# Top-k attention followed by a gated MLP on one core: the attention pipeline one slot shorter, with work moved between VectorE, ScalarE and GpSimd

## The chip, the cores and the metric

The kernel runs on one core of one Trainium2 chip. The metric is the device time of one execution in microseconds (us). The kernel before takes 1711.28 us, the median of three runs that lie between 1711.02 and 1712.13 us. A profile is one further execution, taken by the hardware profiler. The engines are named as in it: PE is TensorE (PEld its weight loads), DVE is VectorE, ACT is ScalarE, POOL is GpSimd, and SP is the queue that issues all DMAs.

## What is computed

Eight batches of eight heads; 576 queries and keys of 64 elements for each head. For every query row only the scores that reach the 32nd largest one count. The result, 4608 rows of 512, goes through a two-layer MLP with the quick GELU. Cut to what matters:

```python
scores = scale * np.matmul(q, k.transpose(0, 1, 3, 2))
kth = np.partition(scores, -top_k, axis=-1)[..., -top_k:-top_k + 1]   # top_k = 32
scores = np.where(scores >= kth, scores, -1000000000.0)
attn = np.exp(scores - np.max(scores, axis=-1, keepdims=True))
attn = attn / (np.sum(attn, axis=-1, keepdims=True) + 1e-09)
o = np.matmul(attn, v)                 # (B,H,S,D) -> x: (B*S, H*D) = 4608 x 512
h = x @ w_in                           # 512 x 2048
g = h * (1.0 / (1.0 + np.exp(-1.702 * h)))
out = g @ w_out                        # 2048 x 512
```

The two weight matrices arrive as 64-bit floats. The kernel turns them into 32-bit floats itself ("rounding" below) from the two 32-bit words of each number; the rest is 32-bit float throughout.

## The kernel before

**Slots.** The attention is cut into 144 slots (`slots`, line 211). A slot is one block of 128 query rows for a pair of heads; each batch has 16 full slots (four row blocks by four head pairs) and two tail slots that share the last 64 rows of two head pairs. The function `slot(n)` (line 445) writes out by hand the order in which every engine gets its work; each engine runs its own queue strictly in that order, and engines wait for each other through semaphores. One call mixes several stages of different slots:

- `scores(n+1)`: PE multiplies queries by keys into `s_ps`, ACT copies the result to `sc` (128 rows, two heads, 576 scores each).
- `topk(n)`: 14 DVE operations, four rounds of "eight largest" (line 245) and three rounds of "remove them" (line 248), each for the two heads. Positions in this list are counted as `i` = 0 to 13 in `slot`.
- `bounds(n-1)`: POOL makes two tiny tiles from the largest and the 32nd largest score. `exponentials(n-1)`: ACT masks the scores (Prelu, line 273), then takes Exp with a running sum `den` (line 275).
- `divide(n-1)`: DVE computes 1/`den` (`some`, `rden`, lines 283 and 285) after position `i` = 5 of `topk(n)`; POOL multiplies the two heads' rows by it (line 288).
- `turn_main(n-2)`, `turn_ends(n-2)`: PE transposes the probabilities in nine blocks into `tp` (line 297), ACT copies them to `pt` (line 298). `values(n-2)`: PE multiplies by V into `o` (line 320), ACT copies to `xT`.
- `prepare`: PE transposes a head pair's queries or keys (lines 199 and 205), ACT copies them to `q_t` or `k_t` (lines 201 to 208). The tables `READY`, `FETCH` and `VALUES` say in which slot of a batch each one is due; around the start of a batch a key pair and the next query pair fall into one slot, twice in each batch from the second on.

**MLP.** When four head pairs of a row block are done, the block joins the list `ready`. Each slot then does a quarter of a block's MLP: `hidden` (16 matmuls, line 361, into the one buffer `ph`), `tanh` on ACT (line 378), `gate` on DVE at the end of the slot's queue (line 385), and in the next slot `project` (four matmuls, line 399), which after four quarters is copied out by ACT (`ob`, line 404) and stored. After the last slot the remaining quarters run alone.

**Weights.** The two weight matrices are loaded and rounded in 32 pieces of 128 by 512 during the first slots: two before slot 0, then three a slot (`by_slot`, line 419). Per piece ACT makes `more` and `size` (lines 133 and 134), DVE runs `cut` (line 137), `sign` (line 142) and `normal` (line 149), and POOL adds the low part (line 146). `cut` and `sign` are put between the operations of `topk(n)`, `normal` after its ninth.

**Buffers.** The tiles `tp` and `o` share two buffers in PSUM (`ps_t`), `s_ps` has two, `ph` and `po` one each. A pool hands out its buffers in turn, so the third `tp` or `o` in program order waits until the first has been copied out.

Of the kernel before, what the change touches and what calls it, by code (L numbers as in the profile page):

```python
# [8 lines left out]
AF = mybir.ActivationFunctionType  # L9
ALU = mybir.AluOpType  # L10
ENG = mybir.EngineType
F32 = mybir.dt.float32
U32 = mybir.dt.uint32
I32 = mybir.dt.int32
PSUM = bass.MemoryType.PSUM

P = 128
TOPK = 32
LOWEST = -3.4028234663852886e38

LEAST_HIGH = 2.0**-15 * 1.125

HUGE = 2.0**100

# [2 lines left out]
def kernel(  # L27
# [24 lines left out]
    nc = tc.nc  # L52
# [11 lines left out]
    G = 4  # L64
    NG = FC // G
    PIECE = 512
    NPIECE = CC * DFF // PIECE + FC
# [6 lines left out]

    const = ctx.enter_context(tc.tile_pool(name="const", bufs=1))
    pool = lambda name, bufs, **kw: ctx.enter_context(tc.tile_pool(name=name, bufs=bufs, **kw))
    raws = pool("raws", 5)
    temps = pool("temps", 3)
    loads = pool("loads", 2)
    vals = pool("vals", 6)  # L80
    qkt = pool("qkt", 5)
# [3 lines left out]
    small = pool("small", 4)  # L85
# [2 lines left out]
    xtt = pool("xtt", 1)  # L88
    gtp = pool("gtp", 3)
    thp = pool("thp", 2)  # L90
    osp = pool("osp", 2)
    ps_s = pool("ps_s", 2, space=PSUM)
    ps_t = pool("ps_t", 2, space=PSUM)
    ps_h = pool("ps_h", 1, space=PSUM)
# [22 lines left out]
    def round_piece(n):  # L117

        c, g = pieces[n]
        dst = wout[:, g, :] if c is None else win[:, c, g * PIECE : (g + 1) * PIECE]
        words = raw.pop(n)[:].rearrange("p (n w) -> p n w", w=2)
        low, high = words[:, :, 0], words[:, :, 1]
        bits = dst.bitcast(U32)  # L130
        more = temps.tile([P, PIECE], I32, name="more")
        size = temps.tile([P, PIECE], F32, name="size")
        nc.scalar.mul(out=more[:], in_=low, mul=2.0**-29)
        nc.scalar.activation(size[:], high.bitcast(F32), AF.Abs)

        def cut():
            nc.vector.tensor_scalar(  # L137
                bits, high, 3, 0x3FFFFFF8, op0=ALU.logical_shift_left, op1=ALU.bitwise_and
            )

        def sign():
            nc.vector.scalar_tensor_tensor(  # L142
                out=bits, in0=high, scalar=0xC0000000, in1=bits, op0=ALU.bitwise_and, op1=ALU.bitwise_or
            )
            whole = dst.bitcast(I32)
            nc.gpsimd.tensor_tensor(out=whole, in0=whole, in1=more[:], op=ALU.add)

        def normal():
            nc.vector.scalar_tensor_tensor(  # L149
                out=dst, in0=size[:], scalar=LEAST_HIGH, in1=dst, op0=ALU.is_ge, op1=ALU.mult  # L150
            )

        return [cut, sign], normal


    qT, kT, vv = {}, {}, {}
# [58 lines left out]
    N = len(slots)  # L215
    PER = N // B
    st = [{} for _ in slots]
# [41 lines left out]
    def bounds(n):  # L259

        top = st[n]["top"]
        cut = st[n]["cut"] = small.tile([P, 2], F32, name="cut")
        low = st[n]["low"] = small.tile([P, 2], F32, name="low")
        nc.gpsimd.tensor_scalar(cut[:], top[:, :, TOPK - 1], -1.0, None, op0=ALU.mult)  # L264
        nc.gpsimd.tensor_tensor(out=low[:], in0=top[:, :, TOPK - 1], in1=top[:, :, 0], op=ALU.subtract)

    def exponentials(n):

        sc, cut, low = st[n]["sc"], st[n]["cut"], st[n]["low"]
        pr = st[n]["pr"] = prp.tile([P, 2 * S], F32, name="pr")  # L270
        den = st[n]["den"] = small.tile([P, 2], F32, name="den")
        for i in range(2):
            nc.scalar.activation(sc[:, i, :], sc[:, i, :], AF.Prelu, bias=cut[:, i : i + 1], alpha=HUGE)  # L273
        for i in range(2):
            nc.scalar.activation(  # L275
                pr[:, i * S : (i + 1) * S], sc[:, i, :], AF.Exp, bias=low[:, i : i + 1],
                accum_out=den[:, i : i + 1],
            )

    def divide(n):  # L280
        den, pr = st[n]["den"], st[n]["pr"]
        some = small.tile([P, 2], F32, name="some")
        nc.vector.tensor_scalar_add(some[:], den[:], 1e-9)
        rden = small.tile([P, 2], F32, name="rden")
        nc.vector.reciprocal(rden[:], some[:])  # L285
        for i in range(2):
            on = pr[:, i * S : (i + 1) * S]
            nc.gpsimd.tensor_scalar(on, on, rden[:, i : i + 1], None, op0=ALU.mult)  # L288

    def turn(n, first, cols, blocks):  # L290
        pr = st[n]["pr"]
# [8 lines left out]
    def turn_main(n):  # L300
        for i in range(2):
            turn(n, i * NF, MAIN[i], NF)

    def turn_ends(n):

        turn(n, 2 * NF, FULL, 1)
# [39 lines left out]

    ready = []
    hidden_at = {"g": 0}
    to_gate, to_project = [], []
    proj = {}  # L350

    def hidden():
# [19 lines left out]

    def tanh():

        if to_gate and len(to_gate[-1]) == 3:
            ph, g, rows = to_gate.pop()
            th = thp.tile([P, G, P], F32, name="th")
            nc.scalar.activation(th[:], ph[:], AF.Tanh, scale=0.851)  # L378
            to_gate.append((ph, g, rows, th))

    def gate():
        if to_gate:
            ph, g, rows, th = to_gate.pop()
            gT = gtp.tile([P, G, P], F32, name="gT")
            nc.vector.scalar_tensor_tensor(  # L385
                out=gT[:], in0=th[:], scalar=1.0, in1=ph[:], op0=ALU.add, op1=ALU.mult
            )
            to_project.append((gT, g, rows))

    def project():  # L390
        if not to_project:
            return
        gT, g, rows = to_project.pop(0)
        if g == 0:
            proj["po"] = ps_p.tile([P, C], F32, name="po")
        po = proj["po"]
        for i in range(G):
            f = g * G + i
            nc.tensor.matmul(  # L399
                po[:], lhsT=gT[:, i, :], rhs=wout[:, f, :], start=(f == 0), stop=(f == FC - 1)  # L400
            )
        if g == NG - 1:
            ob = osp.tile([P, C], F32, name="ob")
            nc.scalar.mul(out=ob[:], in_=po[:], mul=0.5)
            for on, row in rows:
                nc.sync.dma_start(out[row : row + on.stop - on.start, :], ob[on, :])
# [4 lines left out]
    def at(n, fn, *args):  # L411
        later.setdefault(n, []).append((fn, args))
# [3 lines left out]
    READY = ((-6, -5), (-2, -1), (-1, 0), (0, 1))  # L416
    FETCH = ((-12, -11), (-9, -8), (-5, -4), (-1, 0))
    VALUES = (-8, -7, 1, 2)
    by_slot = {-1: [0, 1]}
    for x in range(2, NPIECE):  # L420
        by_slot.setdefault((x - 2) // 3, []).append(x)
    for hp in range(NP):
        for name in "qk":
            at(max(hp - 2, -1), load, name, 0, hp)
            at(hp - 1, prepare, name, 0, hp)
        if hp == 0:
            for x in by_slot[-1]:
                at(-1, load_piece, x)
    for hp in range(NP):
        at(hp - 1, load_v, 0, hp)  # L430
    for n in range(NPIECE // 3):
        for x in by_slot[n]:
            at(n - 1, load_piece, x)
    for b in range(1, B):
        for hp in range(NP):
# [1 line left out]
                at(b * PER + FETCH[hp][i], load, name, b, hp)  # L437
                at(b * PER + READY[hp][i], prepare, name, b, hp)
            at(b * PER + VALUES[hp], load_v, b, hp)
    rounding, last = {}, []  # L440

    def begin_rounding(n):
        rounding[n] = [round_piece(x) for x in by_slot.get(n, [])]

    def slot(n):
        todo = later.pop(n, [])
        for fn, args in todo:
            if fn is not prepare:
                fn(*args)
        if 0 <= n - 1 < N:  # L450
            bounds(n - 1)
            exponentials(n - 1)
        if 0 <= n - 2 < N:
            turn_main(n - 2)
        hidden()
        if 0 <= n - 2 < N:
            turn_ends(n - 2)
        for fn, args in todo:
            if fn is prepare:
                fn(*args)  # L460
        tanh()
        if n + 1 < N:
            scores(n + 1)
        if 0 <= n - 2 < N:
            values(n - 2)
        project()
        if n == -1:
            begin_rounding(-1)
        begin_rounding(n + 1)
        chain = topk(n) if 0 <= n < N else [lambda: None] * 14  # L470
        some = rounding.pop(n)
        first = [op for ops, _ in some for op in ops]
        last.extend(op for _, op in some)
        for i, op in enumerate(chain):
            op()
            if i == 5 and 0 <= n - 1 < N:
                divide(n - 1)
            if i and first:
                first.pop(0)()
            elif last and i > 8:  # L480
                last.pop(0)()
        while first:
            first.pop(0)()
        while last and n >= 0:
            last.pop(0)()
        gate()

    with tc.manual_schedule():
        for n in range(-1, N + 2):
            slot(n)  # L490
        n = N + 2
        while ready or to_project:
            slot(n)
            n += 1

# [29 lines left out]
```

## Time and profile before

| what | value |
|---|---|
| three runs, median | 1711.28 us |
| the profiled execution, its own time | 1710.55 us |
| span of the profiled execution | 1708.6 us |
| granted TensorE clock, mean | 0.97 |
| DVE busy | 1581.2 us (93%) |
| ACT busy | 989.5 us (58%) |
| POOL busy | 595.1 us (35%) |
| DVE "eight largest", lines 245 | 864 and 288 operations of some 746 ns |
| DVE "remove", line 248 | 864 operations of 742 ns |
| DVE gate, line 385 | 144 operations of 671 ns |
| POOL division, line 288 | 288 operations of 1723 ns |
| ACT Prelu and Exp, lines 273 and 275 | 288 each, 767 and 761 ns |

Busy times of an engine overlap little but not never: an operation's duration includes a fixed part that the next one can hide, so the distance between two starts is shorter than a duration (a DVE "eight largest" starts 0.67 us after the one before). The span runs from the first to the last recorded instruction; the execution's own time is 1.95 us longer.

### The profile page before, as it was taken

The page shows a single profiled execution, that of the slowest core. Times are in us where ns is not written, and L with a number is a line of the kernel's source. Part 1 is how long each engine was busy: PE and PEld are TensorE (multiplying, and loading weights), DVE is VectorE, ACT ScalarE, POOL GpSimd, SP SyncE. Part 2 cuts the span into 40 slices and gives each one's busy share as a digit, 9 for nine tenths or more (in the row PEclk, how much of TensorE's full clock was granted, in tenths as well). Part 3 has the DMA queues.
Part 4 walks back from the last instruction along what each step waited for, and adds up shares of the span by engine and source line. Part 5 has one row for each costly group of instructions (what it writes and reads, how often), then busy time and mean ns, then how long its engine had stood idle before and what let it go on. Part 6 is the DMA issues. An engine that isn't in the chain of part 4 may idle for free.

```text
span 1708.6 us, 31456 instructions
## 1 busy us (share of the span) xinstructions
PE 1604.8 (94%) x11824; PEld 1183.7 (69%) x11824; DVE 1581.2 (93%) x3408; ACT 989.5 (58%) x2149; POOL 595.1 (35%) x620
## 2 busy tenths in 40 slices
PE   3447899899999999999999999999999999999998
PEld 2336677577777777777777777777777777777776
DVE  7999999999999999999999999999999999899940
ACT  5655566556665566556665566556665565655530
POOL 3454333333323333333333333333333333233320
PEclk8568999999999999999999999999999999999999
DMA  8232001101000101011000101010010100000000
GB/s 234 93 108 78 20 21 29 42 1 28 21 21 21 35 21 35 14 35 29 21 21 21 35 21 35 14 35 21 21 29 21 35 21 21 22 7 8 7 7 13
DMA packets 125718, 56.54 MB, mean 33 GB/s; under 512 B 116864, under 2 KB 116864, under 8 KB 125568
## 3 DMA queue, kind: packets, MB, share of 16 engines
q1 hardware_dynamic: 125568, 54.55, 12.2%
q8 instruction: 93, 1.52, 0.4%
q14 instruction: 57, 0.47, 0.1%
HBM read 45.09 MB, written 9.44 MB: 32 GB/s over the span
## 4 chain that ended last, share of the span: by engine, by line
PE 87%; DVE 11%; SPq 1%; ACT 1%; issue 0%; DMA 0%; DVEq 0%
PE po L399 29%; PE ph L361 29%; PE o L320 10%; PE s_ps L229 9%; PE tp L297 8%; DVE top L245 4%; DVE left L248 3%; PE tp L199 2%; DVE wout L149 1%; DVE wout L142 1%; DVE win L149 1%; DVE win L137 1%; ACT k_t L201 0%; DVE wout L137 0%; DVE win L142 0%
## 5 line engine op out<-in xcount | busy, mean ns | idle before, releaser
L288 POOL TENSOR_SCALAR pr<-pr,rden 128x576 f32<-128x576 f32 x288 | 493.0, 1723 | 688.1 <-DVE rden L285 427.0
L245 DVE MAX8 top<-left 128x8 f32<-128x576 f32 x864 | 610.1, 746 | 0.0
L399 PE MATMUL po<-wout,gT 128*128 128x512 f32 x1152 | 532.0, 605 | 0.0
L361 PE MATMUL ph<-xT,win 128*128 128x128 f32 x4096 | 489.5, 279 | 18.4 <-DVE gT L385 18.4
L361 PEld LDWEIGHTS ph<-xT,win 128*128 128x128 f32 x4096 | 478.3, 196 | 20.7 <-DVE gT L385 19.7
L248 DVE MATCH_REPLACE8 left<-top,left 128x576 f32<-128x576 f32 x576 | 423.5, 742 | 0.0
L399 PEld LDWEIGHTS po<-wout,gT 128*128 128x128 f32 x1152 | 207.1, 189 | 229.0 <-issue 227.7
L273 ACT ACTIVATE sc<-sc,cut 128x576 f32<-128x576 f32 x288 | 207.3, 767 | 207.0 <-POOL cut L264 207.0
L298 ACT COPY pt<-tp 128x512 f32<-128x512 f32 (+1 forms) x432 | 188.7, 470 | 227.6 <-PE tp L297 227.2
L297 PEld LDWEIGHTS tp<-ident,pr 128*128 128x128 f32 x1296 | 157.3, 143 | 129.4 <-issue 62.1
L297 PE MATMUL tp<-ident,pr 128*128 128x128 f32 x1296 | 195.1, 278 | 50.6 <-ACT pt L298 37.7
L275 ACT ACTIVATE pr<-sc,low 128x576 f32<-128x576 f32 x288 | 218.8, 761 | 0.0
L248 DVE MATCH_REPLACE8 left<-top,sc 128x576 f32<-128x576 f32 x288 | 211.7, 742 | 0.0
L245 DVE MAX8 top<-sc 128x8 f32<-128x576 f32 x288 | 203.5, 747 | 0.9
L236 ACT COPY sc<-s_ps 128x576 f32<-128x576 f32 x288 | 170.4, 645 | 55.2 <-PE s_ps L229 53.2
L229 PE MATMUL s_ps<-k_t,q_t 64*128 64x288 f32 (+1 forms) x1280 | 187.4, 440 | 0.9 <-ACT k_t L201 0.9
L320 PEld LDWEIGHTS o<-pt,v_l 128*64 128x64 f32 x2560 | 130.2, 139 | 57.5 <-ACT th L378 36.3
L320 PE MATMUL o<-pt,v_l 128*64 128x128 f32 (+1 forms) x2560 | 164.4, 272 | 0.0
L385 DVE SCALAR_TENSOR_TENSOR gT<-th,ph 128x512 f32<-128x512 f32 x144 | 96.6, 671 | 54.1 <-ACT th L378 53.8
L264 POOL TENSOR_SCALAR cut<-top 128x2 f32<-128x2 f32 x144 | 31.9, 222 | 304.5 <-DVE top L245 304.5
L229 PEld LDWEIGHTS s_ps<-k_t,q_t 64*128 64x128 f32 (+1 forms) x1280 | 102.1, 181 | 41.0 <-issue 20.6
L378 ACT ACTIVATE th<-ph 128x512 f32<-128x512 f32 x144 | 87.1, 605 | 35.6 <-PE ph L361 35.6
(41 smaller groups left out, 786.0 us busy)
## 6 DMA issues: line engine op xcount, KB each, us to landing
q_l<-in_q_dram SPq DMA_DIRECT2D x64, 128.0 KB, 2.5
k_l<-in_k_dram SPq DMA_DIRECT2D x64, 128.0 KB, 2.5
raw<-in_moe_w_in_dram SPq DMA_DIRECT2D x16, 512.0 KB, 4.2
v_l<-in_v_dram SPq DMA_DIRECT2D x64, 128.0 KB, 2.5
raw<-in_moe_w_out_dram SPq DMA_DIRECT2D x16, 512.0 KB, 3.8
out_dram<-ob SPq DMA_DIRECT2D x32, 256.0 KB, 2.1
ends<-in_q_dram SPq DMA_DIRECT2D x32, 32.0 KB, 2.2
ends<-in_k_dram SPq DMA_DIRECT2D x32, 32.0 KB, 2.3
```

What stands on the lines that cost most here:

```text
L229: nc.tensor.matmul(ps[i][rows, c, 0:HALF], lhsT=qT[b, hps[p]][on, cols], rhs=kT[b, hps[p]][on, FIRST[i] + c * HALF : FIRST[i] + (c + 1) * ...
L236: nc.scalar.copy(out=sc[:, i, :].rearrange("p (c k) -> p c k", c=2), in_=ps[i][:, :, 0:HALF])
L245: nc.vector.max(top[:, i, 8 * r : 8 * r + 8], (left if r else sc)[:, i, :])
L248: nc.vector.match_replace(left[:, i, :], top[:, i, 8 * r : 8 * r + 8], (left if r else sc)[:, i, :], LOWEST)
L273: nc.scalar.activation(sc[:, i, :], sc[:, i, :], AF.Prelu, bias=cut[:, i : i + 1], alpha=HUGE)
L275: nc.scalar.activation(pr[:, i * S : (i + 1) * S], sc[:, i, :], AF.Exp, bias=low[:, i : i + 1], accum_out=den[:, i : i + 1],)
L288: nc.gpsimd.tensor_scalar(on, on, rden[:, i : i + 1], None, op0=ALU.mult)
L297: nc.tensor.transpose(tp[:, c * P : (c + 1) * P], pr[:, cols + c * P : cols + (c + 1) * P], ident[:])
L298: nc.scalar.copy(out=to, in_=tp[:, 0 : blocks * P])
L320: nc.tensor.matmul(o[j * D : (j + 1) * D, 0 : cols.stop - cols.start], lhsT=main[:, c, j, :] if c < NF else tail[:, j, :], rhs=pt[:, j * N ...
L361: nc.tensor.matmul(ph[:, i, :], lhsT=win[:, c, f * P : (f + 1) * P], rhs=xT[:, c, :], start=(c == 0), stop=(c == CC - 1),)
L399: nc.tensor.matmul(po[:], lhsT=gT[:, i, :], rhs=wout[:, f, :], start=(f == 0), stop=(f == FC - 1))
```

## The change

The pipeline loses one slot: transposes and `values` handle slot n-1 instead of n-2, and the order inside `slot` is rewritten. `exponentials(n)` now stands at the end of slot n, and the inversion of `den` after position 8 of `topk(n+1)`. The multiplication by 1/`den` moves from POOL to ACT. `gate` moves from DVE to POOL as two operations, on copies of both factors that ACT makes. `normal` is dropped: `size` is bounded below by a POOL operation first, and `cut` reads it instead of the raw word; the low part is written over the raw piece. Pieces go four a slot for six slots, then three for two. `prepare` of the first batch is one slot earlier, and in every slot it follows `scores`. `project` is split in two halves around `turn_ends`.

```diff
-LEAST_HIGH = 2.0**-15 * 1.125
+LEAST_HIGH = 2.0**-15
...
-    raws = pool("raws", 5)
-    temps = pool("temps", 3)
+    raws = pool("raws", 6)
+    temps = pool("temps", 4)
...
-    osp = pool("osp", 2)
+    osp = pool("osp", 1)
...
-        more = temps.tile([P, PIECE], I32, name="more")
         size = temps.tile([P, PIECE], F32, name="size")
-        nc.scalar.mul(out=more[:], in_=low, mul=2.0**-29)
+        nc.scalar.mul(out=low.bitcast(I32), in_=low, mul=2.0**-29)
         nc.scalar.activation(size[:], high.bitcast(F32), AF.Abs)
+        nc.gpsimd.tensor_scalar(size[:], size[:], LEAST_HIGH, None, op0=ALU.max)
         def cut():
             nc.vector.tensor_scalar(
-                bits, high, 3, 0x3FFFFFF8, op0=ALU.logical_shift_left, op1=ALU.bitwise_and
+                bits, size[:].bitcast(U32), 3, 0x3FFFFFF8, op0=ALU.logical_shift_left, op1=ALU.bitwise_and
             )
...
-            nc.gpsimd.tensor_tensor(out=whole, in0=whole, in1=more[:], op=ALU.add)
-        def normal():
-            nc.vector.scalar_tensor_tensor(
-                out=dst, in0=size[:], scalar=LEAST_HIGH, in1=dst, op0=ALU.is_ge, op1=ALU.mult
-            )
-        return [cut, sign], normal
+            nc.gpsimd.tensor_tensor(out=whole, in0=whole, in1=low.bitcast(I32), op=ALU.add)
+        return [cut, sign]
...
-            nc.gpsimd.tensor_scalar(on, on, rden[:, i : i + 1], None, op0=ALU.mult)
+            nc.scalar.activation(on, on, AF.Copy, scale=rden[:, i : i + 1])
...
+            h = thp.tile([P, G, P], F32, name="h")
+            nc.scalar.copy(out=h[:], in_=ph[:])
...
-            nc.vector.scalar_tensor_tensor(
-                out=gT[:], in0=th[:], scalar=1.0, in1=ph[:], op0=ALU.add, op1=ALU.mult
-            )
+            nc.gpsimd.tensor_tensor(out=gT[:], in0=th[:], in1=h[:], op=ALU.mult)
+            nc.gpsimd.tensor_tensor(out=gT[:], in0=gT[:], in1=h[:], op=ALU.add)
...
-        for i in range(G):
+        for i in range(part * G // 2, (part + 1) * G // 2):
...
+    RATES = (2, 4, 4, 4, 4, 4, 4, 3, 3)
...
-            at(max(hp - 2, -1), load, name, 0, hp)
-            at(hp - 1, prepare, name, 0, hp)
+            at(max(hp - 3, -1), load, name, 0, hp)
+            at(max(hp - 2, -1), prepare, name, 0, hp)
```

The body of `slot` after the change (it replaces lines 446 to 486; `invert` is the part of `divide` that makes `rden`):

```python
        before = 0 <= n - 1 < N
        chain = topk(n) if 0 <= n < N else [lambda: None] * 14
        more = rounding.pop(n, [])
        for i, op in enumerate(chain):
            op()
            if i and more:
                more.pop(0)()
            if i == 8 and before:
                invert(n - 1)
        for op in more:
            op()
        if before:
            divide(n - 1)
        if n == -1:
            for args in preparing[:2]:
                prepare(*args)
            del preparing[:2]
        if n + 1 < N:
            scores(n + 1)
        for args in preparing:
            prepare(*args)
        hidden()
        if before:
            turn_main(n - 1)
        tanh()
        project(0)
        if before:
            turn_ends(n - 1)
        project(1)
        if n == -1:
            for op in begin_rounding(-1):
                op()
        rounding[n + 1] = begin_rounding(n + 1)
        if before and n <= len(by_slot):
            values(n - 1)
        if 0 <= n < N:
            bounds(n)
            exponentials(n)
        gate()
        if before and n > len(by_slot):
            values(n - 1)
```

More of the change, by code (lines that the diff above doesn't have):

```diff
@@ L278, in exponentials, with invert, divide @@
             )
-    def divide(n):
-        den, pr = st[n]["den"], st[n]["pr"]
+    def invert(n):
+        den = st[n]["den"]
         some = small.tile([P, 2], F32, name="some")
         nc.vector.tensor_scalar_add(some[:], den[:], 1e-9)
-        rden = small.tile([P, 2], F32, name="rden")
+        rden = st[n]["rden"] = small.tile([P, 2], F32, name="rden")
         nc.vector.reciprocal(rden[:], some[:])
+    def divide(n):
+        pr, rden = st[n]["pr"], st[n]["rden"]
         for i in range(2):
             on = pr[:, i * S : (i + 1) * S]
-            nc.gpsimd.tensor_scalar(on, on, rden[:, i : i + 1], None, op0=ALU.mult)
+            nc.scalar.activation(on, on, AF.Copy, scale=rden[:, i : i + 1])
     def turn(n, first, cols, blocks):
@@ L348 @@
     hidden_at = {"g": 0}
-    to_gate, to_project = [], []
+    to_gate, gated, to_project = [], [], []
     proj = {}
@@ L373, in tanh @@
     def tanh():
-        if to_gate and len(to_gate[-1]) == 3:
+        if to_gate:
             ph, g, rows = to_gate.pop()
@@ L378, in tanh, with project @@
             nc.scalar.activation(th[:], ph[:], AF.Tanh, scale=0.851)
-            to_gate.append((ph, g, rows, th))
+            h = thp.tile([P, G, P], F32, name="h")
+            nc.scalar.copy(out=h[:], in_=ph[:])
+            gated.append((th, h, g, rows))
     def gate():
-        if to_gate:
-            ph, g, rows, th = to_gate.pop()
+        if gated:
+            th, h, g, rows = gated.pop()
             gT = gtp.tile([P, G, P], F32, name="gT")
-            nc.vector.scalar_tensor_tensor(
-                out=gT[:], in0=th[:], scalar=1.0, in1=ph[:], op0=ALU.add, op1=ALU.mult
-            )
+            nc.gpsimd.tensor_tensor(out=gT[:], in0=th[:], in1=h[:], op=ALU.mult)
+            nc.gpsimd.tensor_tensor(out=gT[:], in0=gT[:], in1=h[:], op=ALU.add)
             to_project.append((gT, g, rows))
-    def project():
-        if not to_project:
+    def project(part):
+        if not to_project or (part and not proj.get("begun")):
             return
-        gT, g, rows = to_project.pop(0)
-        if g == 0:
+        gT, g, rows = to_project[0]
+        if g == 0 and part == 0:
             proj["po"] = ps_p.tile([P, C], F32, name="po")
+        proj["begun"] = True
         po = proj["po"]
-        for i in range(G):
+        for i in range(part * G // 2, (part + 1) * G // 2):
             f = g * G + i
@@ L401, in project @@
             )
+        if part == 0:
+            return
+        to_project.pop(0)
+        proj["begun"] = False
         if g == NG - 1:
@@ L418 @@
     VALUES = (-8, -7, 1, 2)
-    by_slot = {-1: [0, 1]}
-    for x in range(2, NPIECE):
-        by_slot.setdefault((x - 2) // 3, []).append(x)
+    RATES = (2, 4, 4, 4, 4, 4, 4, 3, 3)
+    by_slot, x = {}, 0
+    for n, rate in enumerate(RATES, -1):
+        by_slot[n] = list(range(x, x + rate))
+        x += rate
+    assert x == NPIECE
     for hp in range(NP):
         for name in "qk":
-            at(max(hp - 2, -1), load, name, 0, hp)
-            at(hp - 1, prepare, name, 0, hp)
+            at(max(hp - 3, -1), load, name, 0, hp)
+            at(max(hp - 2, -1), prepare, name, 0, hp)
         if hp == 0:
@@ L430 @@
         at(hp - 1, load_v, 0, hp)
-    for n in range(NPIECE // 3):
+    for n in range(len(by_slot) - 1):
         for x in by_slot[n]:
@@ L439 @@
             at(b * PER + VALUES[hp], load_v, b, hp)
-    rounding, last = {}, []
+    rounding = {}
     def begin_rounding(n):
-        rounding[n] = [round_piece(x) for x in by_slot.get(n, [])]
+        return [op for x in by_slot.get(n, []) for op in round_piece(x)]
     def slot(n):
         todo = later.pop(n, [])
+        preparing = [args for fn, args in todo if fn is prepare]
         for fn, args in todo:
@@ L449, in slot @@
                 fn(*args)
[L450 to L461, printed above, removed]
+        before = 0 <= n - 1 < N
+        chain = topk(n) if 0 <= n < N else [lambda: None] * 14
+        more = rounding.pop(n, [])
+        for i, op in enumerate(chain):
+            op()
+            if i and more:
+                more.pop(0)()
+            if i == 8 and before:
+                invert(n - 1)
@@ L462, in slot @@
+        for op in more:
+            op()
+        if before:
+            divide(n - 1)
+        if n == -1:
+            for args in preparing[:2]:
+                prepare(*args)
+            del preparing[:2]
         if n + 1 < N:
             scores(n + 1)
-        if 0 <= n - 2 < N:
-            values(n - 2)
-        project()
-        if n == -1:
[L468 to L485, printed above, removed]
+        for args in preparing:
+            prepare(*args)
@@ L486, in slot @@
+        hidden()
+        if before:
+            turn_main(n - 1)
+        tanh()
+        project(0)
+        if before:
+            turn_ends(n - 1)
+        project(1)
+        if n == -1:
+            for op in begin_rounding(-1):
+                op()
+        rounding[n + 1] = begin_rounding(n + 1)
[4 more added lines that the diff above has]
+            exponentials(n)
         gate()
+        if before and n > len(by_slot):
+            values(n - 1)
@@ L488 @@
     with tc.manual_schedule():
-        for n in range(-1, N + 2):
+        for n in range(-1, N + 1):
             slot(n)
-        n = N + 2
-        while ready or to_project:
+        n = N + 1
+        while ready or to_project or gated:
             slot(n)
```

## The prediction

> **What bounds the kernel now.** I read the page's busy times and slices first, then the windows, then the chain of waits.
>
> ```profile
> PE 1604.8 (94%) x11824; PEld 1183.7 (69%) x11824; DVE 1581.2 (93%) x3408; ACT 989.5 (58%) x2149; POOL 595.1 (35%) x620
> ...
> PE   3447899899999999999999999999999999999998
> ...
> PE 87%; DVE 11%; SPq 1%; ACT 1%; issue 0%; DMA 0%; DVEq 0%
> ```
>
> Two engines look full, but the chain that ended last runs 87% over PE: once PE is full (from the fifth slice), it decides. Only before that is there time to win. The windows (PE, PEld, DVE, ACT and POOL busy; clock; DMA):
>
> ```profile
> 50.00:100.00 50.00, 22.60 (x120) 15.86 (x120) 49.90 (x98) 30.59 (x64) 25.05 (x22) 0.57 0.30 95
> 100.00:150.00 50.00, 33.92 (x204) 27.30 (x205) 49.90 (x97) 29.57 (x58) 24.64 (x22) 0.75 0.35 107
> ...
> 800.00:1000.00 200.00, 199.12 (x1502) 147.23 (x1501) 192.54 (x422) 120.20 (x264) 68.58 (x73) 1.00 0.10 24
> ```
>
> Early on DVE is full (top-k plus rounding) and PE half empty; later PE has 0.9 us to spare in 200. The chain of waits shows the turn and one PE slot, from `hidden` to `hidden`:
>
> ```profile
> 179.85 5.47 PE ph L361 x32
> 185.43 1.17 PE s_ps L229 x8
> 186.60 1.24 PE o L320 x20
> 187.84 3.63 PE po L399 x8
> 191.47 0.87 PE tp L297 x8
> 192.34 3.57 PE ph L361 x32
> ```
>
> A PE slot is 1.17 + 1.24 + 3.63 + 0.87 + 3.57 + 0.11 (the ninth transpose) = 10.6 us. DVE needs 14 top-k steps of 0.67 or 0.73 (9.7), 0.3 for the inversion and 0.6 for the gate: also 10.6. So the 87 us of gate starts (144 x 0.60) that leave DVE are worth nothing while PE needs 10.6; without that cover they would be worth 0.6 a slot.
>
> **Term 1, the start.** Before, the first top-k starts at 15.3 and a slot with three pieces takes 16.2 us (31.4, 47.6, 63.8), until `hidden` of slot 10 starts at 179.85; from there PE runs to 1704.1, so 1524.3 us are left. After the change one ACT queue carries, in order, division, score copies, transposed blocks, and only then the reading of the next pieces. Durations:
>
> ```profile
> 69.98 1.27 POOL L146 TENSOR_TENSOR win<-win,more 128x512 int32<-128x512 int32 x1 [1.69 <-DVE win L142]
> 70.43 0.85 DVE L283 TENSOR_SCALAR some<-den 128x2 f32<-128x2 f32 x1
> ...
> 71.39 0.41 DVE L137 TENSOR_SCALAR win<-raw 128x512 uint32<-128x512 uint32 x1
> 71.67 1.73 POOL L288 TENSOR_SCALAR pr<-pr,rden 128x576 f32<-128x576 f32 x1 [0.43 <-ACT sc L236]
> ...
> 72.44 0.68 DVE L142 SCALAR_TENSOR_TENSOR win<-raw,win 128x512 uint32<-128x512 uint32 x1
> ```
>
> Count from one inversion (time 0). 0.45 until `rden` is there; division 2 x 0.68 (the Prelu rows' spacing); score copies 1.1; block copies 1.1 and 0.3: ACT is free at 4.3. Each piece then takes 2 x 0.6, so the first `size` is there at 5.5. The new POOL maximum has no row. Nearest is L288, 1.73 for 576 elements, so 1.5 for 512; the low end is the 0.41 of L137, the same form on DVE. I take 1.5: the first `cut` can start at 7.1, while DVE, with five top-k steps (3.45) and the next slot's two (1.35), is there at 5.2. It waits 1.9. Then four cuts at 0.32, four signs at 0.6 and seven top-k steps (4.9) give 8.6. Some 1.8 go to the port: the row at 70.43 shows `some` taking 0.85 instead of 0.15 because a two-input POOL operation was under way, and three cuts or signs meet POOL's additions with 0.6 each. Period: 7.1 + 8.6 + 1.8 = 17.5 us for four pieces; with a maximum of 0.4, 16.2. In slots 6 and 7 one piece less (-1.6) and the tanh and copy ahead of the pieces (+1.1), with the gate's two POOL operations in the way, about cancel. POOL's `bounds` now queue behind the four maxima (to 12), exponentials end at 15.8, in time for the next inversion at 17.5.
>
> The first top-k comes later: pieces 0 and 1 now pass ACT behind the second pair's copies (k lands at 12.8, so about 15.1), then two pairs of ACT reads, POOL and two cuts and signs: 20.5, not 15.3. SP also issues 3.5 us of extra q and k loads ahead of the next four pieces, which delays slot 0 by some 2 us. Slot 0 takes 17, eight steps and four pieces of slot 1 another 12.4: first inversion at 50, the one in slot 7 at 50 + 6 x 17.5 = 155. From the transposes 1.5 us behind it PE has enough to do. What is left is the 1524.3 and what the old kernel had already done at 179.85: one `hidden` (3.6), two scores (2.3), three turns (2.9), two values (2.6), two projects (6.9), 18.3 together. Chain end 156.5 + 1524.3 + 18.3 = 1699.1, against 1704.1; the end pays 0.6, since the gate on POOL (2 x 1.27, after 1.1 on ACT) outlasts the 3.44 of the project before it. **Term 1: -4.4 us** (-14 with the short maximum).
>
> The Trainium skill weighs the maximum otherwise. GPSIMD Engine Reference, section "Engine selection", calls one-input operations roughly line-rate; at its 1.2 GHz 512 elements would be an estimated 0.43 us, and the sum would be that of the short maximum. The division's row, 1.73 us for 576, is four times that. SBUF — State Buffer, section with "The single rule", says that a DVE operation with two SBUF inputs waits for a GpSimd operation that reads SBUF; the row at 72.44 shows L142, two inputs, taking its usual 0.68 inside the division. By the rule two signs a slot would wait up to 1.5, an estimated 20 us against the change.
>
> **Term 2, PE in the long part.** Division on ACT (2 x 0.68) and the copy of `ph` (0.5) bring ACT from 6.9 to 8.8 of 10.6 us, covered by PE; POOL's 1.27 x 2 likewise. But ACT's order puts exponentials behind the transposed ends. In a PE slot from its scores on, the ends are transposed at 7.3, copied at 7.8; Prelu 1.35 and Exp 1.52 end at 10.7.
>
> ```profile
> 916.05 0.19 ACT L275 ACTIVATION_READ_ACCUMULATOR pr<-sc,low 128x1 f32 x1
> ...
> 916.27 0.17 DVE L283 TENSOR_SCALAR some<-den 128x2 f32<-128x2 f32 x1 [1.05 <-ACT pr L275]
> 916.48 0.17 DVE L285 RECIPROCAL rden<-some 128x2 f32<-128x2 f32 x1
> ```
>
> 0.5 from `den` to `rden`: division ends at 12.5, which is 1.95 into the next slot, score copies at 3.05. The transposes of that slot come at 4.74, so an ordinary slot stays at 10.6. A slot that prepares k and the next q does not: q needs a third `tp` buffer, free when `k_t` is copied.
>
> ```profile
> 273.96 0.60 ACT L201 ACTIVATE k_t<-tp 128x512 f32<-128x512 f32 x1 [0.17 <-PE tp L199]
> ...
> 274.61 0.66 PE L199 MATMUL tp<-ident,q_l 128*128 128x128 f32 x4 [0.44 <-ACT k_t L201]
> ```
>
> Before, ACT took it at once and PE lost 0.44. After, `k_t` is copied behind division and scores, at 3.7, and PE wants the buffer at 1.9: 1.8 lost, with `hidden` and everything of PE queued behind. Twice in each of seven batches: 14 x (1.8 - 0.44) = 19. Where `ob` ran in the slot before (four of them), exponentials and division come 2.05 later: +8. The pair ahead of the two slots without `hidden` (near 313 before) is partly absorbed: -3. **Term 2: +24 us**, ends 0 (ACT is early after all) and +45 (all 14 as late as those behind an `ob`). Cutting `project` in two adds a change of weights after a short matmul; before, such a change costs 0.1 (3.63 against 3.44 for eight, in the tail). As many others go: 0, ends -14 and +14 (0.1 x 144).
>
> `osp` with one buffer: `ob` comes every fourth slot, its store lands in 2.1 us; nothing.
>
> **Sum.** 1708.6 - 4.4 + 24 = 1728.2 span. The median is 2.7 above the span: **1731 us**.
>
> **Rivals.** *Faster: the key copy is on time.* If exponentials are done a good us earlier than I reckon, the 14 stalls stay at 0.44 and only the start counts: 1731 - 24 = 1707, with the short maximum 1697. It decides where the net of the stalls is under 4 us. For it: the early slices show PE half empty, DVE loses a third of its rounding work. Against: ACT's strict order. *The port.* The gate ends on POOL about 0.5 before `some` starts; if it is 0.5 longer, `some` waits up to 0.7 (the row at 70.43), DVE has 0.65 spare in a slot, and each further us costs 137: with 0.5 a slot 1731 + 69 = 1800. Against: every other DVE operation then is a one-input top-k step, which POOL does not slow (746 ns in all stretches). *The start is not shorter at all:* if cuts also wait for the maxima, period 19, start +9 rather: 1742. *Cancelling:* stalls of 0.8 each and the start as reckoned: within 0.2%, about what a measurement of this kernel can tell from no change.
>
> **Chances.** Forecast 0.47 (1716 to 1748, the ends of the maximum, half of term 2's and the weight changes), faster rival 0.30 (1694 to 1707), port 0.08, longer start 0.08, cancelling 0.07. Faster 0.30, same 0.07, slower 0.63. Range 1694 to 1748: it leaves out the port and little else.
>
> **What will show it.** Right: DVE idle before L137 from POOL's maximum, some 2 us a slot, and `some` to `some` near 17 us early on; PE full from about 157; L194's query matmuls waiting for ACT `k_t` with some 25 us over 14 times or so. Wrong: `k_t` waits under 10 us in total (faster rival); DVE `some` long and PE waiting for `sc` in ordinary slots (port); a PE slot that isn't 10.6 us.

## The result and the profile after

The changed kernel takes 1753.88 us (median of four runs, 1752.2 to 1754.66), the kernel before 1711.18 beside it: a ratio of 1.0247, 95% interval 1.0229 to 1.0265. It is slower, as forecast, but by 42.7 us instead of 20, and above the range. The profiled execution spans 1750.4 us against 1708.6.

The page of the changed kernel: busy times, PE's slices and granted clock, and engines on the chain that ended last.

```profile
PE 1607.2 (92%) x11824; PEld 1172.6 (67%) x11824; DVE 1482.7 (85%) x3232; ACT 1231.8 (70%) x2581; POOL 515.2 (29%) x652
...
PE   3346998999999998999989999999989999999998
...
PE 81%; DVE 8%; ACT 6%; issue 2%; POOL 1%; DMA 0%; SPq 0%; POOLq 0%; ACTq 0%
```

DVE lost 98 us of work, and the time did not fall. ACT now has 6% of the chain; and PE's row, nearly solid from the fifth slice on before, is thinner up to the fourth and has eights spread over the rest. Two windows of the same kernel (PE, PEld, DVE, ACT and POOL busy; clock; DMA):

```profile
100.00:150.00 50.00, 23.82 (x148) 19.32 (x149) 45.17 (x84) 29.29 (x58) 31.46 (x28) 0.64 0.34 102
...
800.00:1000.00 200.00, 194.34 (x1465) 142.00 (x1465) 177.99 (x395) 148.81 (x314) 52.80 (x72) 0.99 0.11 27
```

From 100 to 150 PE did 23.8 us where it did 33.9 before, and DVE, full before, is idle for 5. In the long part PE is idle for 5.7 us in 200; it was 0.9. So there are two losses, an early and a spread one. PE's waits (engine, tile and line, what it waited for: total, times, longest), of the changed kernel:

```profile
PE tp L194 <- ACT k_t L196: 31.3, 14, 2.6
...
PE tp L194 <- ACT xT_t L335: 4.5, 4, 1.1
```

Before, the same wait was 6.6 in the same 14 places, and there was none for `xT_t`:

```profile
PE tp L199 <- ACT k_t L201: 6.6, 14, 0.6
```

The early loss shows on DVE:

```profile
DVE win L137 <- POOL size L134: 23.4, 4, 17.9
DVE wout L137 <- POOL size L134: 13.3, 4, 4.4
```

DVE stands 36.7 us before the first `cut` of a slot, waiting for POOL's maximum (17.9 of it before the first top-k). The chain of waits between two inversions of the changed kernel shows why the maximum is late:

```profile
72.46 0.09 DVE some L278
...
72.83 1.44 ACT pr L286 x2
74.28 1.06 ACT sc L231 x2
75.34 0.50 ACT pt L296
...
76.56 0.67 ACT raw L132
77.22 0.57 ACT size L133
...
77.94 1.50 POOL size L134
...
79.46 0.04 DVE win L137
...
90.65 0.09 DVE some L278
```

On ACT the division, the score copies and the transposed blocks come first, the reading of the pieces after them, POOL's maximum after that, and only then can DVE cut: 7.0 us behind the inversion. The next inversion comes 18.2 us after this one.

### The profile page after: what moved, and what is told of

It is laid out like the page before. It is cut to its first block, busy times and chain, and to the rows that moved or that the text cites. A ratio compares the mean times of both kernels' runs of the same rounds, so it can differ in the third digit from the quotient of the medians.

```text
span 1750.4 us, 31703 instructions
## 1 busy us (share of the span) xinstructions
PE 1607.2 (92%) x11824; PEld 1172.6 (67%) x11824; DVE 1482.7 (85%) x3232; ACT 1231.8 (70%) x2581; POOL 515.2 (29%) x652
## 4 chain that ended last, share of the span: by engine, by line
PE 81%; DVE 8%; ACT 6%; issue 2%; POOL 1%; DMA 0%; SPq 0%; POOLq 0%; ACTq 0%
PE ph L359 29%; PE po L399 27%; PE o L318 8%; PE tp L295 8%; PE s_ps L224 8%; DVE left L243 3%; DVE top L240 3%; ACT pr L286 2%; PE tp L194 2%; ACT pr L270 1%; ACT sc L231 1%; POOL size L134 1%; DVE wout L137 1%; ACT sc L268 1%; DVE win L137 1%
## 5 line engine op out<-in xcount | busy, mean ns | idle before, releaser
L240 DVE MAX8 top<-left 128x8 f32<-128x576 f32 x864 | 621.8, 747 | 0.0
L359 PE MATMUL ph<-xT,win 128*128 128x128 f32 x4096 | 498.0, 281 | 0.0
L296 ACT COPY pt<-tp 128x512 f32<-128x512 f32 (+1 forms) x432 | 194.0, 482 | 232.4 <-PE tp L295 231.0
L399 PEld LDWEIGHTS po<-wout,gT 128*128 128x128 f32 x1152 | 198.1, 192 | 183.0 <-issue 181.7
L286 ACT ACTIVATE pr<-pr,rden 128x576 f32<-128x576 f32 x288 | 207.6, 768 | 139.9 <-DVE rden L280 139.9
L385 POOL TENSOR_TENSOR gT<-th,h 128x512 f32<-128x512 f32 x144 | 183.5, 1275 | 391.4 <-ACT h L378 391.4
L295 PE MATMUL tp<-ident,pr 128*128 128x128 f32 x1296 | 199.1, 282 | 63.3 <-ACT pr L286 61.3
L386 POOL TENSOR_TENSOR gT<-gT,h 128x512 f32<-128x512 f32 x144 | 184.2, 1279 | 11.3
L278 DVE TENSOR_SCALAR some<-den 128x2 f32<-128x2 f32 x144 | 23.1, 161 | 168.1 <-ACT pr L270 168.1
```

The costliest lines, as they stand in the source:

```text
L240: nc.vector.max(top[:, i, 8 * r : 8 * r + 8], (left if r else sc)[:, i, :])
L286: nc.scalar.activation(on, on, AF.Copy, scale=rden[:, i : i + 1])
L295: nc.tensor.transpose(tp[:, c * P : (c + 1) * P], pr[:, cols + c * P : cols + (c + 1) * P], ident[:])
L296: nc.scalar.copy(out=to, in_=tp[:, 0 : blocks * P])
L359: nc.tensor.matmul(ph[:, i, :], lhsT=win[:, c, f * P : (f + 1) * P], rhs=xT[:, c, :], start=(c == 0), stop=(c == CC - 1),)
L386: nc.gpsimd.tensor_tensor(out=gT[:], in0=gT[:], in1=h[:], op=ALU.add)
```

## The experiments

The times are medians of four executions (of ten for the first experiment and for the gate alone); the kernel before, run beside each of the three groups of experiments, took 1710.92, 1710.92 and 1709.46. A ratio is to that kernel, with its 95% interval.

**The query transposes behind `hidden`.**

```diff
-        for args in preparing:
+        behind = preparing[1:] if n >= 8 else []
+        for args in preparing[: len(preparing) - len(behind)]:
             prepare(*args)
         hidden()
+        for args in behind:
+            prepare(*args)
```

> The changed kernel with one edit: from slot 8 on, the query transposes that share a slot with key transposes are issued behind the 16 matmuls of `hidden` instead of ahead of them. Theory (the key copy): PE loses 31.3 us in 14 waits for ACT `k_t` (2.24 each), 24.7 more than before, and runs a few us of matmuls at a lower clock after each; the edit gives ACT 5.4 us more, so the waits fall below 5 us in all and the time falls by 26 to 36, from 1754 to 1718 to 1728. Rival A (the gate on POOL or the division on ACT makes every slot a little longer): no change, within 4 us. Rival B (the stall only moves on: the transposes of probabilities behind it then wait for the tp buffer of the query copy): 31 us of waits turn up under another name, and the time falls by less than 10.

1712.71 us; ratio to the kernel before 1.0010 (1.0001 to 1.0020). 41 us came back, 5 more than the theory's upper end, and this by moving four transposes in 14 places. The `k_t` waits are gone, and the wait that replaces them (for `q_t`) is small. Kernel with the edit:

```profile
PE tp L295 <- ACT q_t L196: 3.5, 14, 0.3
```

Rivals A and B fall. What the theory had too small is the clock. The changed kernel around one of its longer waits, then the same place with the edit, each time the transposes of q and `hidden` (start, duration, idle before):

```profile
291.11 1.11 PE L194 MATMUL tp<-ident,q_l 128*128 128x128 f32 x4 [2.64 <-ACT k_t L196]
292.02 4.85 PE L359 MATMUL ph<-xT,win 128*128 128x128 f32 x32
```

```profile
287.74 3.74 PE L359 MATMUL ph<-xT,win 128*128 128x128 f32 x32
291.31 0.60 PE L194 MATMUL tp<-ident,q_l 128*128 128x128 f32 x4
```

From 291.5 to 295 the granted clock was 0.59 in the changed kernel and 1.00 with the edit. Over the 14 places of the changed kernel, eight `hidden` took 4.7 to 5.4 us instead of 3.74, 11.0 us together, and three groups of q transposes 0.45 more each: 12.4. With 31.3 of waits less the 3.5 that replace them that is 40.2, and from the transposes at which PE becomes full to the end the two spans differ by 40.0 (1583.4 against 1543.4).

**Only in one of the two slots.** Each batch but the first has two slots that prepare keys and queries. The edit above with `n % PER == 0` (the second of them; `PER` is the number of slots in a batch, 18) or `n % PER == PER - 1` (the first) added to the condition:

> The changed kernel with the query transposes behind `hidden` only in the second of the two slots of each batch that prepare keys and queries (the one whose wait is 2.6 us and after which `hidden` took 4.6 to 4.9 us instead of 3.7). Theory (these seven waits cost 2.6 each and 1.5 more through a lower clock, 29 of the 40 us that the full edit saved): 1754 - 29 = 1725, 1722 to 1729. Rival (the fall in clock belongs to both slots, or to something else): half of the full edit, 1731 to 1736.

> The changed kernel with the query transposes behind `hidden` only in the first of those two slots (the one whose wait is 1.9 us, with `hidden` at its usual length behind it). Theory: seven times 1.9, less the 0.25 of the wait that comes in its place, 11 to 12 us: 1740 to 1744. Rival (equal shares, or a clock that falls behind these waits too): 1731 to 1736.

1731.10 (ratio 1.0129, 1.0110 to 1.0147) and 1735.36 (1.0150, 1.0135 to 1.0165): nearly equal shares, by the medians in the rivals' bounds (the first only just, and its four runs spread from 1727.88 to 1735.94). The premise was wrong: I had read the first such batch alone. The longer waits (2.6) follow an `ob`. In the second slot of four batches it ran 7 us ahead, in the slot before. In the first slot of three batches it ran 17 us ahead, two slots back: there the `ob` made the exponentials late, DVE's `some` waited 2.59 for them (at 662.79 in the changed kernel), and so the next inversion, division and `k_t` came late too. Ahead of the seven shorter waits the last `ob` lies 32 to 37 us back. So 15.3 and 16.0 us of waits are left. The price of the waits stands: in the kernel with the second slot mended, 14.2 us of waits net and five of the eight slow `hidden` are gone, 21.7 together, and its span is 21.9 shorter. Over the three kernels, `hidden` was slow behind 13 of the 14 waits of 2.6 us, and behind 2 of the 14 of 1.8 to 1.9.

**All transposes ahead of the division.** Here nothing moves past `hidden`; ACT's order changes:

```diff
+        if n >= 8:
+            for args in preparing:
+                prepare(*args)
+            preparing = []
         if before:
             divide(n - 1)
```

> The changed kernel with one edit: from slot 8 on, all transposes of queries and keys, and so ACT's copies of them, stand ahead of the division and the scores instead of behind them; nothing moves past `hidden`. Theory (the copy of `k_t` is late because ACT's own order puts division and score copies, 2.5 us, in front of it): the waits for `k_t` fall from 31.3 us to 5 to 12 in all, and the time falls to 1714 to 1726. Rival (it is the place on PE's queue that counts, with ACT busy anyway by exponentials at that moment): waits of 20 us or more stay, and the time stays above 1735.

1741.16 (1.0178, 1.0163 to 1.0193): the theory's waits with the rival's time. PE's waits in this kernel:

```profile
PE tp L194 <- ACT xT_t L335: 11.9, 14, 2.3
PE tp L194 <- ACT k_t L196: 7.7, 14, 0.6
```

So ACT's order did make `k_t` late: put first, it waits 0.55. But PE now reaches the key transposes before its 1.2 us of scores, and behind a tail slot it meets the copies of `xT_t`, which stand on ACT behind the exponentials. So 24 us of waits for `k_t` went and 7 for `xT_t` came. Four of the latter are 2.3 long, and behind three of these the clock fell again: `hidden` took 4.9 to 5.2 there, the scores ahead of it 2.3 instead of 1.2. The kernel is only 13 us faster; how the rest divides was not worked out.

**The pieces read earlier.**

```diff
         for op in more:
             op()
+        if n >= 1:
+            rounding[n + 1] = begin_rounding(n + 1)
         if before:
             divide(n - 1)
...
-        rounding[n + 1] = begin_rounding(n + 1)
+        if n < 1:
+            rounding[n + 1] = begin_rounding(n + 1)
```

> The changed kernel with one edit: from slot 1 on, ACT's reading of the next slot's pieces and POOL's maxima stand ahead of the division and the score copies instead of behind the transposed blocks. Theory (the start is no shorter because the maxima come late on ACT's queue): DVE's waits for `size` (23.4 and 13.3 us in the changed kernel) fall by more than half, the distance from one inversion to the next falls from 18.2 us to 16 or 17, and the time falls by 7 to 15, from 1754 to 1739 to 1747. Rival (DVE's operations themselves, the port and the extra piece fill the 18 us): within 3 us of 1754. Second rival (division and transposes, now later by the reading, become what DVE waits for through `den`): DVE's waits move to `some`, and the time rises.

1730.27 (1.0112, 1.0097 to 1.0127), 23.6 less; the theory had 7 to 15. DVE is full; the kernel with the edit:

```profile
100.00:150.00 50.00, 37.64 (x234) 27.65 (x236) 49.90 (x99) 34.05 (x68) 38.17 (x34) 0.81 0.26 74
...
145.07 1.32 PE L295 MATMUL tp<-ident,pr 128*128 128x128 f32 x8 [1.25 <-ACT pr L286]
```

An inversion follows the last by 15.6 us, not 18.2, with four pieces in between. PE's last wait for a division in the start ended at 145.1; in the changed kernel it ended at 167.0 (7.25 long). That is 21.9 of the 22.2 us between the spans.

**No maximum.** The line with the POOL maximum is left out, and with it the lower bound of `size`:

```diff
-        nc.gpsimd.tensor_scalar(size[:], size[:], LEAST_HIGH, None, op0=ALU.max)
```

> The changed kernel without the POOL maximum (the lower bound on `size` is left out; everything else stays). Theory A (the maximum of 1.5 us and its queue of four, behind a late ACT, are what DVE waits for): the first top-k comes 2 us earlier, each of the seven slots after it gets 1.5 to 2.5 us shorter, and the time falls by 12 to 18, from 1754 to 1736 to 1742. Theory B (ACT's late reading alone sets the time of the first `cut`): one slot's first `cut` comes 1.5 us earlier but the fourth waits for ACT, and the time falls by less than 8.

1734.77 (1.0148, 1.0133 to 1.0163), 19.1 less: theory A, a little above its upper end. With the maximum gone DVE still waits for ACT's `size`, 24.5 us in all instead of 36.7. Reading earlier, with the maximum, gives 4 to 6 us more than leaving it out; what the maximum costs where it is in time was not tried.

**The old pieces in the new order.** Three VectorE operations a piece and three pieces a slot, as in the kernel before, with its `round_piece`, buffers and `last` list:

```diff
-    RATES = (2, 4, 4, 4, 4, 4, 4, 3, 3)
+    RATES = (2,) + (3,) * 10
...
+            elif last and i > 8:
+                last.pop(0)()
```

> The changed kernel with the weight pieces as before: three VectorE operations a piece, no POOL maximum, three pieces a slot in ten slots. Everything else (shorter pipeline, division on ACT, gate on POOL) stays. Theory (two operations and four pieces a slot do save DVE time, most of which the late maxima take back): DVE is full with 16.2 us a slot but needs two slots more, so PE is full 5 to 15 us later than at 167, and the time is 1757 to 1770. Rival (the POOL maximum costs more than the dropped operation saves): PE is full at 155 to 162, and the time falls to 1742 to 1749. In both the 14 waits for `k_t` stay at 31 us.

1742.62 (1.0186, 1.0171 to 1.0201): the rival's time. As the changed kernel places it, the new rounding costs 11 us. The rival's date for a full PE fell, though: the last long wait of the start ends at 176.5, but PE has done more work early on (117.9 us in the first 200, against 102.3).

**The new pieces in the old kernel.** The diff's `round_piece`, rates and buffers in the kernel before, the maxima issued behind the slot's additions and division:

```diff
-        begin_rounding(n + 1)
         chain = topk(n) if 0 <= n < N else [lambda: None] * 14
...
+        begin_rounding(n + 1)
         gate()
```

> The kernel before with one part of the change: the weight pieces in two VectorE operations, with the POOL maximum and four pieces a slot; division stays on POOL, the gate on DVE, the old pipeline and slot order; the maxima are issued behind the slot's division and additions. Theory (the new rounding is a gain wherever the maxima are in time, and was a loss only behind the new ACT order): a slot of four pieces takes about as long as the old slot of three, two such slots fall away, and the time falls by 8 to 25, from 1711 to 1686 to 1703. Rival (POOL, with 5.9 us of maxima, 5.1 of additions and 3.5 of division a slot, becomes the bound of the start): 1708 or more.

1699.87 (0.9944, 0.9927 to 0.9961): theory, 9.6 us faster than before. The same rounding gains 12.3 in the new order once the pieces are read early (1742.62 to 1730.27).

**Gate and division alone, in the old kernel.** The gate as two POOL operations on ACT's copies; and, in another kernel, the division by ACT:

```diff
-            nc.gpsimd.tensor_scalar(on, on, rden[:, i : i + 1], None, op0=ALU.mult)
+            nc.scalar.activation(on, on, AF.Copy, scale=rden[:, i : i + 1])
```

> The kernel before with one part of the change: the gate leaves DVE and is two POOL operations on copies made by ACT (and the output tile has one buffer). Theory (PE needs 10.6 us a slot with or without it): 0 to +2, 1711 to 1713, the small loss at the end where the gate outlasts a project. Rival A (DVE decides in the long part, its 144 x 0.60 count): 15 us or more faster. Rival B (POOL's two-input operations hold up DVE, or the gate comes too late for the project): 10 us or more slower.

> The kernel before with one part of the change: the division runs on ACT (Copy with a scale by row) instead of on POOL; its place in the program stays behind position 5 of the top-k steps. Theory (the place of an operation on ACT's queue matters, not its load): the old order has two slots between exponentials and transposes, so ACT's 1.36 us more a slot are covered; 1710 to 1715. Rival (ACT's load or DVE's waits for it cost in every slot): 1725 or more.

The gate: 1710.41 (0.9998, 0.9989 to 1.0008). DVE's busy time falls from 1581 to 1500 us and POOL's rises to 957, for nothing: PE covers it. Both rivals fall. The division: 1764.12 (1.0313, 1.0297 to 1.0328), 53 us slower, where the theory had at most 4. The trace of that kernel in a slot with `ob`:

```profile
842.09 0.60 ACT L404 ACTIVATE ob<-po 128x512 f32<-128x512 f32 x1 [3.36 <-PE po L399]
...
842.58 1.43 ACT L288 ACTIVATE pr<-pr,rden 128x576 f32<-128x576 f32 x2
843.40 1.32 PE L297 MATMUL tp<-ident,pr 128*128 128x128 f32 x8 [1.35 <-ACT pr L288]
```

In the old order the output copy stands ahead of the division on ACT. It waits for PE's last `project`, so in every fourth slot the division starts when PE already wants its result: 34 waits of 1.35 and two of some 1.05 come to 48 us of the 53; the other 5 were not followed. ACT was busy 67% of the span. It was again the place on the queue and not the load, but the slot of slack that I had credited the old order with isn't there.

**Both edits, and an earlier start.** First the two edits together; then also the two pieces that stand ahead of the first top-k moved into slot 0:

```diff
-    RATES = (2, 4, 4, 4, 4, 4, 4, 3, 3)
+    RATES = (0,) + (4,) * 8
...
-            if i and more:
+            if i > (0 if n else 6) and more:
```

> The changed kernel with both edits together: the query transposes behind `hidden` from slot 8 on, and ACT's reading of the next pieces ahead of division and score copies from slot 1 on. Theory (two independent losses, one in the first 170 us and one spread over the seven later batches): the two gains add, 1754 - 41 - 23.5 = 1689, within 4. Rival (both come from one thing, ACT's lateness, so that the second edit finds part of its gain already taken): 1696 to 1706.

> Both edits, and the two pieces that are cut ahead of the first top-k step move into slot 0 (four pieces in each of slots 0 to 7, in slot 0 from the eighth step on; the loads of a head pair as late as in the kernel before). Theory (the first top-k, whose scores are there at 11.1 us, waits until 21.3 for `size` of these pieces and their cuts, and from then on DVE is full): the first top-k starts at 11 to 13 and the time falls by 5 to 9 below that with both edits alone, to 1680 to 1684. Rival (the pieces' arrival decides, and DVE waits for them in slot 0 instead): within 3 us of the kernel with both edits.

1688.18 (0.9868, 0.9852 to 0.9885): the gains add, to 1 us, so the two losses are independent. With the pieces moved, 1687.37 (0.9863, 0.9848 to 0.9878): no difference, the rival. The first top-k did start at 10.8 instead of 21.4, and the first inversion came 9.1 earlier. But the two pieces now lie in slots 6 and 7, and scores are late there (DVE waits 3.15 us for them at 131.3, their copy standing on ACT behind the reading), so that PE is full at 144.8 against 145.2. Either kernel beats both the changed one and the one before. Of the 23 us against the latter, the new pieces alone give 9.6 (above); the remaining 13 belong, if the parts add, to the rest of the change in its mended order.

## Why the prediction was half right

What it had right, by its own steps:

- "The 87 us of gate starts that leave DVE are worth nothing": the gate alone gave 0.5 us with an interval that spans no change. The ordinary PE slot stayed at 10.6 (`hidden` at 176.22 and 186.83), so the split of `project` cost nothing, and the end paid 0.7 (0.6 forecast).
- The port rival fell: no gate held up `some`. The changed kernel's group has a mean of 161 ns:

```profile
L278 DVE TENSOR_SCALAR some<-den 128x2 f32<-128x2 f32 x144 | 23.1, 161 | 168.1 <-ACT pr L270 168.1
```

- The place, the number and the waiting time of the `k_t` stalls: 14 with 31.3 us against 6.6 before, 24.7 net, where term 2 had 24. The split was off, but not the sum: the forecast was ten of 1.8 and four of 3.85 behind an `ob`. The four took 2.64, three more with the `ob` two slots back, which the prediction did not see, took 2.6, and seven took 1.8 to 1.9. That the sum came out so near is partly luck.
- The maximum: 1.5 us was taken for 512 elements, and 1.509 measured; DVE waited 1.97 for it in the slot at 79.46, with 1.9 forecast.

What failed, against the forecast span of 1728.2 (22.2 us short), is one term of the sum that was too small and one that was missing:

- Term 1, "Period: 7.1 + 8.6 + 1.8 = 17.5 us for four pieces". The 7.1 were exact (7.07). The rest, the part of DVE's own operations, was 11.1 instead of 10.4, because the 1.8 ("some 1.8 go to the port") were too few: in the slot at 79.46 the four `cut` and four `sign` took 6.80 us, 2.44 more than at their usual 0.41 and 0.68, with POOL's work under way. 0.9 of this fell under the maxima, which the prediction had put at nothing after reading one row (the `sign` at 72.44, late in a division). This gives 18.2 in the steady slots. From the inversion in slot 1 to that in slot 2 it took 20.7, because ACT's copies of the last head pair, prepared in slot 1, were not counted ahead of the reading; and the step by which the fewer piece and the tanh and copy in slots 6 and 7 "about cancel" failed, since these took 18.7 and 20.1. With 51.7 instead of 50 for the first inversion the one of slot 7 came at 165.7, not 155, and PE was full at 167.0, not 156.5. So the start term was mis-sized by 10.5: +6 instead of -4.4. The rival "the start is not shorter at all", which got a chance of 0.08, had the period (19.0 in the mean of these six) and part of the reason, with +9 where +6 was measured.
- Term 2, "1.8 lost, with `hidden` and everything of PE queued behind": the sum ended at the wait. What is queued behind also ran at a lower clock for a while, 12.4 us over the eight places. No term stood for that, though the start of the old trace had clocks of 0.57 and 0.75 wherever PE had gaps. 10.5 and 12.4 make 22.9, with 22.2 missing.

The faster rival ("the key copy is on time") was built by experiment: it comes to 1712.7 and not 1707; its start was no shorter (PE full at 167.9). Both losses begin on ACT's strict queue of everybody's copies. In the long part I followed it through most kinds of slot; in the start through one steady slot, and took the others to cancel.

As for the two pages of the Trainium skill that the prediction weighed against the rows: GPSIMD Engine Reference, section "Engine selection", calls one-input operations roughly line-rate, and here they were not, with 1.509 us for 512 elements against the estimated 0.43. SBUF — State Buffer, section with "The single rule", foresaw a hold of `sign` during the maxima. It is there, but for a part of the maximum only (last section).

## What to carry to other kernels

When work moves to an engine with time to spare, read its queue in order and ask who waits for the entry behind the new one. The first link of a chain to other engines belongs ahead of work that can wait: reading the pieces earlier was worth 24 us. Where PE waits for a copy that frees a PSUM buffer, there are two ways, and both were tried: the copy earlier on ACT gave 13 us and a new wait, other matmuls for PE ahead of the place where it waits gave 41. And price a stall of PE with the matmuls behind it, not only with the gap.

## What the hardware showed beyond that

**PE's clock followed its idle time in windows of 3.41 us, not the length of a gap.** In the traces of all 14 kernels the granted clock is 1.00 or 0.50 and changes only on a grid of 3.41 us. The grid lies differently in each run: its first line is 0.80 us behind the start in the changed kernel, 0.33 in the one with only the second slot mended. The wait that ended at 291.11 in the changed kernel, cut along its grid (PE busy, clock, DMA):

```profile
284.11:287.53 3.42, 2.46 (x48) 1.00 0.50 143
287.53:290.94 3.41, 0.77 (x5) 1.00 0.54 121
290.94:294.35 3.41, 3.24 (x15) 0.50 0.32 72
294.35:297.77 3.42, 3.42 (x32) 1.00 0.00 0
```

Over the 14 traces PE was idle, by its records, for more than 1.9 us in 142 windows at full clock, and each of them was followed by a window at half clock. Of the more than 6300 windows with less than 1.77 none was; 25 lie between, and went both ways. This accounts for the odd cases above. The one wait of 2.6 behind which `hidden` kept its length has a grid line in it, with 1.80 us on the larger side (the kernel with the second slot mended; PE, PEld, DVE, ACT and POOL busy, clock, DMA):

```profile
1464.66:1468.07 3.41, 1.61 (x15) 1.61 (x15) 3.41 (x9) 2.67 (x8) 0.38 (x2) 1.00 0.45 101
1468.07:1471.48 3.41, 3.41 (x33) 3.41 (x32) 3.41 (x8) 0.32 (x1) 0.00 (x0) 1.00 0.01 2
```

The two waits of 1.88 behind which it was slow lie whole in one window. So what a gap of 2 to 3 us costs depends also on where the grid falls, and that differs from run to run. What was lost behind such a window is 0.9 to 2.2 us a `hidden`. The Trainium skill, TensorE: Matmul & The Clock Gate, Part 1, gives a window of about 3.4 us that runs on its own, after which an idle engine gets half the clock. The window is there; but it need not be idle throughout: 1.9 us of it were enough here.

**A one-input POOL operation holds up DVE only at its start.** The changed kernel, where POOL's four maxima run from 77.94 at 1.46 us each, so that they start at 77.94, 79.39, 80.84 and about 82.3:

```profile
77.94 5.84 POOL L134 TENSOR_SCALAR size<-size 128x512 f32<-128x512 f32 x4 [4.12 <-ACT size L133]
79.46 0.82 DVE L137 TENSOR_SCALAR win<-size 128x512 uint32<-128x512 uint32 x1 [1.97 <-POOL size L134]
...
80.94 1.06 DVE L142 SCALAR_TENSOR_TENSOR win<-raw,win 128x512 uint32<-128x512 uint32 x1
...
82.65 0.53 DVE L137 TENSOR_SCALAR win<-size 128x512 uint32<-128x512 uint32 x1
```

`cut` and `sign`, normally 0.41 and 0.68, took 0.4 more when they began some 0.1 us behind a maximum's start, and `cut` 0.1 more when it began 0.36 after it. All 21 that began in the first 0.45 us of a maximum in this trace, but for one more told below, ended as if released 0.47 to 0.48 us into it. In the kernel before, a `sign` at 72.44, 0.77 after POOL's division began, took its usual 0.68. The exception went the other way: a `sign` that began at 25.82, only 0.03 behind a maximum, took its usual 0.68, and that maximum 2.23 instead of 1.48. Both forms of DVE operation are held, the one-input `cut` too; a top-k step never was. POOL's two-input additions hold them for longer, almost to their end: a `cut` at 85.07, 0.58 into an addition of 1.28, took 0.99, and a `sign` up to 1.65. Whether the hold sits in the port or elsewhere was not tried.
